# Loading the last pieces of batch 1 in row parts: a linear-attention kernel with a feed-forward layer on one Trainium2 core

## The chip, the cores and the metric

The kernel runs on one core of one Trainium2 chip. The metric is the time of one execution in microseconds (us) on the device; the figure for a kernel is the median of its runs. The profile is one further execution of the same program. Engines are called PE (matrix multiply; PEld is its weight load), DVE, ACT, POOL and SP (which here only issues transfers). "SPq" is SP's queue of transfer requests.

## The reference, cut to what matters

```python
# q, k, v: (batch 8, heads 8, seq 576, head_dim 64), float32
q_s = exp(q) / sum over head_dim          # softmax along d
k_s = exp(k) / sum over seq               # softmax along s
kv  = einsum('bhsd,bhse->bhde', k_s, v)
att = einsum('bhsd,bhde->bhse', q_s, kv)
x   = att.transpose(0, 2, 1, 3).reshape(4608, 512)
h   = x @ w_in                            # 512 -> 2048
g   = h + sin(alpha * h)**2 / alpha
out = g @ w_out                           # 2048 -> 512, float32
```

## The kernel before, in words

**Tiles.** The 4608 tokens are nine tiles `t` of 512. For each tile, `mm_h` (L282) makes sixteen blocks `ni` of 128 hidden features in PSUM, four matmuls for each; `sine` takes sin on ACT (L288) and squares it on ACT, POOL or DVE; `combine` (L298, DVE) adds and writes `g`; `mm_o` (L302) multiplies `g` by `wout`, 64 matmuls for a tile, and `evac_o` copies the result out of PSUM and stores it in two requests of 64 rows each (L317). The order on every engine is written out by hand.

**PSUM banks.** A block of `mm_h` takes the bank that its letter names. For tile 1 the sixteen letters are `"aabb..."` with a change in between:

```python
BANKS = {0: "aabbkllaabbkllaa", 1: "aakbbllaabbllaab", 2: "aabbopaabbopaabb"}
```

Letters a, b and l have two banks each, so the third block with a letter waits until `combine` of the first has read its bank. In tile 1, block 9 (b) so waits for `combine` of block 3, and block 15 (b) for that of block 9.

**Batch 1.** The attention of a batch makes the columns `xT` that `mm_h` reads. Batch 1's inputs are loaded in pieces into staging tiles `st_q`, `st_k`, `st_v` of 128 rows. `load_q1` (L466) loads q in two halves; `load_kv1` (L474) issues k's first half, v's first half, k's second half, and v's second half in two pieces: its first five groups of columns (`j` 0 to 5, 320 KB) and then its last four (256 KB). These five are called k0, v0, k1, v1a and v1b here. After them SP issues `wout_v` rows 14 and 15 into `late_w` (L491, 256 KB each; w14 and w15 here), the ninth q groups of batches 0 and 1 into `q8` (L493, 128 KB each), and then batch 2 with `load_batch(2)` (L99: q, k, v, 1152 KB each).

**Who uses them.** `cast_v1(1)` (L499) casts v1a on POOL and v1b on DVE into `vb`; `wide_mm(1, 1)` (L184) multiplies them with the exponential of k1. L545 casts w14 on POOL and w15 on ACT into `wout`; the last eight `mm_o` of tile 0 (`take(os)`, L553) need them. `exp_to` (L546, recorded at L118) takes the exponential of both parts of `q8` on ACT, and is followed on ACT by a table load (L552), one copy of `evac_o` and the sixteen sines of tile 1. `norm_q8` uses the result on DVE.

**The queue of requests.** All of these requests go through SP in program order. Their completion is told by eight semaphores (`DMAHW0` to `DMAHW7`) that are used in turn, and each request carries a wait on the semaphore that it is to use: it is issued when the request eight places before it has landed. A staging tile or `late_w` tile that is used again adds a wait for its last reader.

Of the kernel before, what the change touches and what calls it, by code (L numbers as in the profile page):

```python
# [23 lines left out]
def kernel(  # L24
# [14 lines left out]
    nc = tc.nc  # L39
    ctx.enter_context(nc.allow_non_contiguous_dma(reason="layout"))  # L40
    B, H, S, D = q.shape
# [3 lines left out]
    J = 9  # L45
# [23 lines left out]
    q8 = singles.tile([128, 4, 2, D], F32, name="q8")  # L69
# [9 lines left out]
    def src_view(t, b):  # L79
        return t[b].rearrange("(i e) (p j) d -> (e p) i (j d)", e=2, j=J)  # L80

    win_v = moe_w_in.rearrange("(c p) n -> p c n", c=4)
    wout_v = moe_w_out.rearrange("(no ni) d -> ni no d", ni=128)
    out_v = out.rearrange("(b p j) d -> b j p d", b=B, j=J)

    staged = {}
# [15 lines left out]
    def load_batch(b):  # L102
        load("q", q, b)
        load("k", k, b)
        load("v", v, b)
# [354 lines left out]
    with ES:  # L460
        def load_q1(ii):
            if ii == 0:
# [3 lines left out]
            nc.sync.dma_start(out=st[:, ii::2, 0:8].rearrange("p i j d -> p i (j d)"),  # L466
                              in_=src_view(q, 1)[:, ii::2, 0:8 * D])

        def load_kv1():
            for n in "kv":  # L470
                staged[n, 1] = stage.tile([128, 4, J, D], F32, name=f"st_{n}", tag="st")
            for n, t, ii, j0, j1 in (("k", k, 0, 0, J), ("v", v, 0, 0, J), ("k", k, 1, 0, J),
                                     ("v", v, 1, 0, 5), ("v", v, 1, 5, J)):
                nc.sync.dma_start(out=staged[n, 1][:, ii::2, j0:j1].rearrange("p i j d -> p i (j d)"),  # L474
                                  in_=src_view(t, 1)[:, ii::2, j0 * D:j1 * D])

        late = {6: lambda: load_q1(0), 8: lambda: load_wout(8, 12), 10: lambda: load_wout(12, 14),
                12: lambda: (load_q1(1), load_kv1())}
        for ni in range(nN):
            h_slot(0, ni, "DPPAPPAPPAAPPAPD"[ni], lag)  # L480
# [6 lines left out]
        os = o_quad(0, accs, [DVE_CP, ACT_CP, DVE_CP, DVE_CP])  # L487

        late_w = [spool.tile([128, MF], F32, name="s") for _ in range(2)]
        for n in range(2):  # L490
            nc.sync.dma_start(out=late_w[n], in_=wout_v[:, 14 + n])  # L491
        for b in range(2):
            nc.sync.dma_start(out=q8[:, :, b], in_=src_view(q, b)[:, :, 8 * D:J * D])  # L493
        load_batch(2)

        def cast_v1(ii):
# [157 lines left out]
    for ni in range(nN):  # L654
# [4 lines left out]
        elif ni in (9, 13):  # L659
            ii = ni // 12  # L660
# [3 lines left out]
    for t in range(3, nT):  # L664
        b = t + 1 if t + 1 < B else None
# [74 lines left out]
```

## Time and profile before

| | |
|---|---|
| runs | 281.94, 282.15, 282.15 us; median 282.15 us |
| the profiled execution's own time | 282.07 us |
| its span, first to last instruction | 280.3 us |
| granted TensorE clock | 0.997 |
| PE busy | 268.7 us |
| ACT, DVE, POOL busy | 224.1, 186.5, 81.1 us |
| moved by transfers | 46.06 MB, mean 164 GB/s |

The span is 1.77 us shorter than the execution's own time; what lies outside it is not part of the instructions. Times inside the profile count from the start of the span. A line of the timeline gives start, duration, engine, line, operation, tiles and, in brackets, how long the engine had been idle before it and what ended that idle time. A line of the waits gives the total, how often, and the longest.

### The profile page before, as it was taken

The page shows a single profiled execution, that of the slowest core. Times are in us where ns is not written, and L with a number is a line of the kernel's source. Part 1 is how long each engine was busy: PE and PEld are TensorE (multiplying, and loading weights), DVE is VectorE, ACT ScalarE, POOL GpSimd, SP SyncE. Part 2 cuts the span into 40 slices and gives each one's busy share as a digit, 9 for nine tenths or more (in the row PEclk, how much of TensorE's full clock was granted, in tenths as well). Part 3 has the DMA queues.
Part 4 walks back from the last instruction along what each step waited for, and adds up shares of the span by engine and source line. Part 5 has one row for each costly group of instructions (what it writes and reads, how often), then busy time and mean ns, then how long its engine had stood idle before and what let it go on. Part 6 is the DMA issues. An engine that isn't in the chain of part 4 may idle for free.

```text
span 280.3 us, 4775 instructions
## 1 busy us (share of the span) xinstructions
PE 268.7 (96%) x1814; PEld 124.9 (45%) x1843; DVE 186.5 (67%) x278; ACT 224.1 (80%) x321; POOL 81.1 (29%) x76
## 2 busy tenths in 40 slices
PE   3999999999999999999999999999999999999994
PEld 1544454444444444444444444444444444444443
DVE  3868877999779767766676677567775555555421
ACT  5799558999588999899989998999877777777400
POOL 2978112778666450026011600350000000000000
PEclk9999999999999999999999999999999999999998
DMA  7999999895698049712971199115001111111143
GB/s 257 313 197 235 291 384 404 269 401 144 140 269 343 0 104 302 301 39 66 328 309 39 40 294 365 44 39 124 18 21 37 37 40 40 41 42 44 39 99 75
DMA packets 39607, 46.06 MB, mean 164 GB/s; under 512 B 17040, under 2 KB 22944, under 8 KB 39584
## 3 DMA queue, kind: packets, MB, share of 16 engines
q1 hardware_dynamic: 33952, 41.11, 46.5%
q0 software_dynamic: 5472, 4.52, 9.7%
q8 instruction: 14, 0.23, 0.3%
q10 hardware_dynamic: 160, 0.13, 0.2%
q14 instruction: 9, 0.07, 0.1%
HBM read 36.71 MB, written 9.44 MB: 165 GB/s over the span
## 4 chain that ended last, share of the span: by engine, by line
PE 83%; DMA 6%; ACT 4%; issue 2%; POOL 1%; SPq 1%; DVE 1%; ACTq 0%
PE hp L282 37%; PE op L302 37%; DMA st_v<-in_v_dram 6%; ACT s L288 2%; PE kvp L173 2%; PE hp L302 2%; PE op L282 1%; PE op L710 1%; PE lp L282 1%; POOL s L292 1%; PE hp L237 1%; PE xp L237 1%; DVE g L298 1%; SPq L474 1%; SPq L327 0%
## 5 line engine op out<-in xcount | busy, mean ns | idle before, releaser
L298 DVE SCALAR_TENSOR_TENSOR g<-s,inva_sb,hp 128x512 bf16<-128x512 f32 x129 | 95.1, 745 | 58.9 <-ACT s L290 53.3
L282 PE MATMUL hp<-xT,win 128*128 128x512 bf16 x508 | 128.6, 379 | 0.5
L302 PE MATMUL op<-wout,g 128*128 128x512 bf16 x463 | 117.6, 379 | 1.7 <-issue 1.3
L288 ACT ACTIVATE s<-hp,alpha_sb 128x512 f32<-128x512 f32 x129 | 86.9, 684 | 21.7 <-PE hp L282 20.3
L282 PEld LDWEIGHTS <-win 128*128 128x128 bf16 x576 | 55.7, 98 | 67.8 <-issue 0.8
L302 PEld LDWEIGHTS <-g 128*128 128x128 bf16 x560 | 53.4, 98 | 65.0 <-issue 2.5
L290 ACT ACTIVATE s<-s 128x512 f32<-128x512 f32 x112 | 70.7, 632 | 3.6
L292 POOL TENSOR_TENSOR s<-s 128x512 f32<-128x512 f32 x28 | 29.5, 1066 | 16.3 <-ACT s L288 16.2
L152 POOL TENSOR_TENSOR qn<-qe,qs 128x1152 bf16<-128x1152 bf16 x11 | 23.2, 2128 | 28.8 <-DVE qs L146 24.4
L137 POOL CAST vb<-st_v 128x1152 bf16<-128x1152 f32 x12 | 14.7, 1258 | 46.1 <-DMA st_v<-in_v_dram 46.1
L314 DVE COPY o<-op 128x512 f32<-128x512 f32 (+2 forms) x32 | 21.1, 660 | 9.7 <-PE op L302 7.4
L118 ACT ACTIVATE qe<-st_q 128x1152 bf16<-128x1152 f32 (+2 forms) x18 | 17.7, 1027 | 6.0 <-DMA st_q<-in_q_dram 5.8
L118 ACT ACTIVATE ke<-st_k 128x1152 bf16<-128x1152 f32 x16 | 17.9, 1153 | 2.6 <-DMA st_k<-in_k_dram 2.6
L145 DVE TENSOR_REDUCE qs<-qe 128x36 f32<-128x2304 bf16 x5 | 12.8, 2551 | 8.3 <-ACT qe L118 8.3
L302 PE MATMUL hp<-wout,g 128*128 128x512 bf16 x45 | 12.0, 379 | 0.2 <-issue 0.2
L118 ACT ACT_TABLE_LOAD x7 | 9.0, 1283 | 0.8 <-PEq L724 0.7
L302 PE MATMUL lp<-wout,g 128*128 128x512 bf16 x32 | 9.2, 379 | 0.1
L371 PE MATMUL warm<-st_q,ident 128*128 128x512 f32 (+1 forms) x6 | 4.4, 871 | 4.5 <-DMA st_q<-in_q_dram 4.5
L282 PE MATMUL lp<-xT,win 128*128 128x512 bf16 x32 | 7.7, 379 | 0.5 <-DMA win<-in_moe_w_in_dram 0.5
L250 DVE CAST xT<-xp 128x1024 bf16<-128x1024 f32 (+1 forms) x7 | 7.4, 1065 | 0.0
L298 DVE SCALAR_TENSOR_TENSOR g<-s,inva_sb,lp 128x512 bf16<-128x512 f32 x8 | 5.7, 740 | 0.4 <-POOL s L292 0.4
L108 POOL DMA_DIRECT2D win<-in_moe_w_in_dram x8 | 5.9, 755 | 0.0
(99 smaller groups left out, 138.2 us busy)
## 6 DMA issues: line engine op xcount, KB each, us to landing
out_dram<-o SPq DMA_DIRECT2D x70, 128.0 KB, 2.4
st_q<-in_q_dram SPq DMA_DIRECT2D x6, 1152.0 KB, 6.6
st_k<-in_k_dram SPq DMA_DIRECT2D x6, 1152.0 KB, 9.2
st_v<-in_v_dram SPq DMA_DIRECT2D x6, 1152.0 KB, 11.5
st_k<-in_k_dram SPq DMA_DIRECT2D x4, 576.0 KB, 8.1
st_q<-in_q_dram SPq DMA_DIRECT2D x4, 512.0 KB, 6.0
wout<-in_moe_w_out_dram POOLq DMA_DIRECT2D x3, 512.0 KB, 11.6
win<-in_moe_w_in_dram POOLq DMA_DIRECT2D x5, 256.0 KB, 6.2
```

Source lines behind the costliest of these rows:

```text
L118: nc.scalar.activation(dst[:, :, ii * 128:(ii + 1) * 128].rearrange("p j (x d) -> p x j d", x=2), src[:, ii::2], AX.Exp)
L137: engs[ii](vv[:, 2 * ii:2 * ii + 2, :, 0:D], staged["v", b][:, ii::2])
L145: nc.vector.tensor_reduce(qs, A["qe", b].rearrange("p j (i d) -> p j i d", i=4), axis=AXL.X, op=ALU.add)
L152: engs[ii % len(engs)].tensor_tensor(qn[:, ii, 0:j1].rearrange("p j (x d) -> p j x d", x=2), qe[:, ii], part.unsqueeze(3).to_broadcast([12 ...
L250: eng(xT[:, c, d0:d0 + m - n], xp[..., n:m])
L282: nc.tensor.matmul(hp, win[:, KO[k], ni * 128:(ni + 1) * 128], xT[:, KO[k], t * MF % NX:t * MF % NX + MF], start=(k == 0), stop=(k == 3))
L288: nc.scalar.activation(s, hp, AX.Sin, scale=alpha_sb[:, ni:ni + 1])
L290: nc.scalar.activation(s, s, AX.Square)
L292: nc.gpsimd.tensor_tensor(s, s, s, op=ALU.mult)
L298: nc.vector.scalar_tensor_tensor(G[t][:, ni], in0=s, scalar=inva_sb[:, ni:ni + 1], in1=hp, op0=ALU.mult, op1=ALU.add)
L302: nc.tensor.matmul(acc, G[t][:, ni, j * 128:(j + 1) * 128], wout[:, ni, :], start=(ni == 0), stop=(ni == nN - 1))
L314: eng(o[:, cols], acc)
```

## The change

Five pieces are requested in two parts each, divided by rows (partitions) where they were one request of 128 rows: v1a in 104 and 24 rows, w14 in 120 and 8, w15 in 56 and 72, the ninth q groups of batch 0 in 88 and 40 and of batch 1 in 63 and 65. The order of the pieces, the bytes and the destinations stay. SP so issues five requests more. An instruction that reads one of these pieces now waits for the semaphores of both parts. The order of instructions on PE, DVE, ACT and POOL is unchanged.

```diff
+        def row_parts(*cuts):
+            at = (0,) + cuts + (128,)
+            return [slice(a, z) for a, z in zip(at, at[1:])]
+
         def load_kv1():
             for n in "kv":
                 staged[n, 1] = stage.tile([128, 4, J, D], F32, name=f"st_{n}", tag="st")
-            for n, t, ii, j0, j1 in (("k", k, 0, 0, J), ("v", v, 0, 0, J), ("k", k, 1, 0, J),
-                                     ("v", v, 1, 0, 5), ("v", v, 1, 5, J)):
-                nc.sync.dma_start(out=staged[n, 1][:, ii::2, j0:j1].rearrange("p i j d -> p i (j d)"),
-                                  in_=src_view(t, 1)[:, ii::2, j0 * D:j1 * D])
+            for n, t, ii, j0, j1, cuts in (("k", k, 0, 0, J, ()), ("v", v, 0, 0, J, ()), ("k", k, 1, 0, J, ()),
+                                           ("v", v, 1, 0, 5, (104,)), ("v", v, 1, 5, J, ())):
+                for r in row_parts(*cuts):
+                    nc.sync.dma_start(out=staged[n, 1][r, ii::2, j0:j1].rearrange("p i j d -> p i (j d)"),
+                                      in_=src_view(t, 1)[r, ii::2, j0 * D:j1 * D])
...
-        for n in range(2):
-            nc.sync.dma_start(out=late_w[n], in_=wout_v[:, 14 + n])
-        for b in range(2):
-            nc.sync.dma_start(out=q8[:, :, b], in_=src_view(q, b)[:, :, 8 * D:J * D])
+        for n, cut in ((0, 120), (1, 56)):
+            for r in row_parts(cut):
+                nc.sync.dma_start(out=late_w[n][r], in_=wout_v[r, 14 + n])
+        for b, cut in ((0, 88), (1, 63)):
+            for r in row_parts(cut):
+                nc.sync.dma_start(out=q8[r, :, b], in_=src_view(q, b)[r, :, 8 * D:J * D])
         load_batch(2)
```

## The prediction

> **What bounds the kernel now.** I read the page first, then the chain of work that ended last around the change (28 to 48 us), then SP's own waits, then the timeline of 38 to 60 us engine by engine, then busy time by windows.
>
> ```profile
> PE 268.7 (96%) x1814; PEld 124.9 (45%) x1843; DVE 186.5 (67%) x278; ACT 224.1 (80%) x321; POOL 81.1 (29%) x76
> ...
> sum 57.00, PE 56.26 PEld 26.34 DVE 48.11 ACT 45.05 POOL 30.18; mean PE 2.68 PEld 1.25 DVE 2.29 ACT 2.15 POOL 1.44
> ```
>
> PE is the bound. The second line is the sum over windows from 27 to 84 us: PE has 0.74 us of idle in 57. So a delay of PE here is not made up later, and a gain is limited to the few tenths that PE waits. The chain shows where it waits:
>
> ```profile
> 29.60 11.16 DMA st_v<-in_v_dram
> 40.76 0.05 issue
> 40.81 0.74 POOL vb L499
> 41.55 0.04 issue
> 41.59 0.77 PE kvp L184 x18
> 42.37 1.00 PE hp L282 x4
> ```
>
> v1a is issued at 29.60 and lands at 40.76; POOL casts it; PE's `wide_mm(1, 1)` starts on that. From 42.37 the chain is PE alone. The rest of the split pieces act on PE through ACT and DVE:
>
> ```profile
> 42.77 0.62 ACT L545 CAST wout<-s 128x512 bf16<-128x512 f32 x1 [0.97 <-DMA s<-in_moe_w_out_dram]
> 43.79 0.82 ACT L118 ACTIVATE qe<-q 128x256 bf16<-128x256 f32 x2 [0.40 <-DMA q<-in_q_dram]
> 48.35 1.41 DVE L298 SCALAR_TENSOR_TENSOR g<-s,inva_sb,hp 128x512 bf16<-128x512 f32 x2 [0.74 <-POOL s L292]
> 51.26 1.39 DVE L298 SCALAR_TENSOR_TENSOR g<-s,inva_sb,hp 128x512 bf16<-128x512 f32 x2
> 50.55 3.62 PE L282 MATMUL hp<-xT,win 128*128 128x512 bf16 x16
> ```
>
> ACT waits for w15, then for `q8`; from 43.79 it has no pause up to tile 1's first sine (46.50), whose square POOL hands to DVE at 48.35; DVE then has no pause either. The pair at 51.26 is `combine` of blocks 3 and 4: block 3 ends at about 51.95. The sixteen matmuls at 50.55 are blocks 7 to 10; one takes 0.216 us, so block 9, which reuses block 3's bank, starts at 52.28. **The margin is 0.33 us** (block 15 on block 9: 57.69 against 57.30, 0.39). If `q8` lands more than 0.33 us later, PE pays the rest.
>
> SP's waits:
>
> ```profile
> SPq L493 <- DMA st_k<-in_k_dram: 2.3, 1, 2.3
> SPq L99 <- DMA st_v<-in_v_dram: 0.7, 1, 0.7
> ```
>
> The second `q8` request stood 2.3 us, until k0 landed at 37.05: it is the eighth after k0. This is the wait of the semaphores used in turn, and the change moves it.
>
> Last, how dear a request of fewer than 128 rows is. The nearest rows are the stores of 64 rows, alone on the queue, against loads of 128 rows:
>
> ```profile
> 122.60:124.10 1.50, 1.50 (x9) 0.69 (x7) 0.38 (x1) 1.50 (x3) 0.00 (x0) 1.00 0.75 175
> 36.00:40.00 4.00, 4.00 (x46) 2.45 (x46) 3.50 (x5) 1.99 (x3) 0.62 (x1) 1.00 1.06 401
> ```
>
> The last two numbers are the transfer engines' busy share and GB/s: 175/0.75 = 233 against 401/1.06 = 378 GB/s for each unit of busy share. A byte in a 64-row request took 1.62 times as long.
>
> **The change, part by part.** The time of each piece on a full queue follows from the landings (issue plus time to landing: 40.76, 41.45, 42.13, 42.75, 43.22, 43.63): v1a 0.87 us after k1 (39.89), w14 0.68, w15 0.62, `q8` 0.47 and 0.41.
>
> *Cost of the parts.* Between nothing (same bytes, queue full) and 0.62 times these: 0.54, 0.42, 0.38, 0.29, 0.25, in all 1.88 us. A gain is the first rival. I take half, 0.31: 0.27, 0.21, 0.19, 0.15, 0.13, in all 0.95 us. Half, because the parts follow one another on a queue where engines are not in step, while the stores stood alone, and the `q8` pieces already move more slowly (131 KB in 0.41 to 0.47 us, against 262 KB in 0.62 to 0.68), which may hide the loss. [...]
>
> *v1a.* One more issue, 0.47 us, is covered: it stands at 29.60 and the queue reaches it near 39.9 (uncovered 0.5 us). Landing +0.27, POOL's cast and `wide_mm` follow: PE +0.27 at 41.59. v1b moves by the same, and with it the second half of `wide_mm`.
>
> *w14, w15.* Their second and later parts now wait for the second half of q (27.65 + 6.7 = 34.35), k0 (37.05) and v0 (38.45); w15 was out at 33.73. The queue reaches w15 after 42: covered by over 3 us. Landing: w14 42.61, w15 43.42 (+0.67). ACT's cast of w15 then ends at 44.07. PE wants w15 at 43.64 + 0.22 + 0.27 = 44.13: just covered.
>
> *q8.* Its four parts wait for k1 (39.89), v1a's two parts, and v1b (41.45 + 0.27 = 41.72). Issues take 0.42 and 0.68 in the trace, so the last is out at about 41.8 to 42.4. Issue to landing is at least 1.8 us in the stores (2.3 median), 43.6 to 44.7; by the queue 43.63 + 0.95 = 44.58. I take 44.58. ACT, POOL and DVE move by 0.95; PE loses 0.95 - 0.33 = 0.62, which contains the 0.27 of v1a (PE waits for the later one). Three further semaphore waits on ACT at 17 ns each (the row of L317's) make 0.05.
>
> *Batch 2.* SP's three requests go out at about 42.4 instead of 38.51, 3.9 us late behind the `q8` waits. q, k and v landed at 46.5, 49.3 and 52.8; ACT first reads q at 61.33 and POOL v at 61.08: 8.3 us of cover for v. The first store, which stood 2.8 us behind them, has no reader; uncovered it would hold an `o` buffer, of which there are four.
>
> Sum: 0.62 + 0.05, rounded to **0.7 us**: 282.07 + 0.7 = 282.8 us for the profiled execution; the median of the runs is 0.08 higher, within the rounding.
>
> **The rivals.**
>
> *The parts leave out a late engine (no change, or faster).* The trace's completion records raise each request's semaphore sixteen times. For v1a fifteen lie between 38.49 and 39.43 and one at 40.76; every request from k0 to `q8` has one such straggler, 0.9 to 1.3 us late. If the straggler has no share of the parts, v1a lands at 39.43 + 0.2 and PE starts `wide_mm` when it is free (41.45 instead of 41.59) and does not pause for DVE's cast (0.06): about -0.2 us, **281.9**. `q8` then lands within its margin. It decides from the point where v1a lands before 40.6. For: the straggler is there, and v1a's landing heads the chain. Against: nothing in the profile says that the parts avoid it, or which engine it is; and PE has only 0.3 us to give. [...]
>
> *The wait in turn decides (slower by more).* If each `q8` issue takes 0.7 us and the last (42.7) lands 2.3 later, at 45.0, PE loses 45.0 - 43.63 - 0.33 = 1.05: **283.1**. A `q8` request in the trace took 6.6 us to land, but behind a full queue; this one would be near its head.
>
> *All is hidden.* The parts cost nothing in a full queue, `q8` lands within 0.33: 282.1 to 282.3.
>
> **How the numbers follow.** A measurement of this kernel can tell about 0.2%, 0.56 us. Forecast 0.50: its spread is 0 to 1.56 us (1.88 - 0.33), so 0.42 slower, 0.08 same. Straggler rival 0.28: 0.19 same, 0.09 faster. Wait in turn 0.12: slower. Hidden 0.08: same. 0.02 for what I do not see, half each way. In all: faster 0.10, same 0.35, slower 0.55. The range goes from the straggler rival with all of PE's 0.3 us (281.8) to the forecast's upper end (283.6). The forecast's own range, by its two bounds, is 282.1 to 283.6.
>
> **What would show it.** Right: v1a's cast on POOL later than 40.81, ACT's exponential of `q8` near 44.7, DVE's first `combine` of tile 1 near 49.3, and a PE wait on DVE between 50 and 58 us that was not there. The straggler rival: POOL's cast before 40.5 and `q8` at or before 43.8. The wait in turn: the last `q8` issue after 42.5 with an empty queue behind it. I am wrong at the root if `q8` is late by over 0.5 us and PE still loses nothing, or if PE loses time outside 38 to 60 us.

## Result and profile after

| | before | changed |
|---|---|---|
| median of nine runs each | 282.02 us (281.64 to 282.28) | 283.94 us (283.27 to 285.9) |
| the profiled execution's own time | 282.07 us | 283.37 us |
| its span | 280.3 us | 281.6 us |
| granted TensorE clock | 0.997 in the profiled execution | 0.998 in the profiled execution; of the nine runs, 0.998 to 1.000 in five, 0.992 to 0.993 in four |

The ratio is 1.0083, interval 1.0067 to 1.0098: slower by 1.9 us, where 0.7 was forecast. The direction was right; the size was not, and the median is 0.34 above the range. The five runs at full clock lie between 283.27 and 283.94, and their median, 283.83, is still 1.81 us above the kernel before; the four others, at 284.76 to 285.9, have no profile, and why their clock is lower stays open.

The page of the changed kernel, in the line of busy times, has no more work on any engine than before (PE's sum differs because matmul records are missing in the trace of before):

```profile
PE 272.3 (97%) x1843; PEld 125.3 (44%) x1843; DVE 186.5 (66%) x278; ACT 223.6 (79%) x321; POOL 80.5 (29%) x76
```

So the time is a wait. The chain that ended last (start, duration, what) shows whose:

```profile
31.46 11.43 DMA st_v<-in_v_dram
42.90 0.02 issue
42.92 0.44 DVE vb L506
43.36 0.04 issue
43.40 0.40 PE kvp L184 x8
43.81 1.00 PE hp L282 x4
```

Before, it came through v1a and POOL's cast; now it comes through v1b, which the change does not touch. `mm_h` goes on at 43.81 instead of 42.37. PE's timeline at this place, with the idle time and its releaser in brackets, first the kernel before, then the changed one:

```profile
41.59 0.77 PE L184 MATMUL kvp<-vb,ke 64*128 64x130 bf16 x18
42.65 0.46 PE L184 MATMUL kvp<-vb,ke 64*128 64x130 bf16 x10 [0.77 <-POOL vb L506]
43.40 0.40 PE L184 MATMUL kvp<-vb,ke 64*128 64x130 bf16 x8 [0.29 <-DVE vb L506]
```

Before, the eighteen matmuls ran in one piece, with 0.10 us of idle ahead of them. The timelines of ACT, POOL and DVE give the landings. Two lines of the kernel before, for k1 and v1b (the prediction shows the others):

```profile
39.91 1.17 ACT L118 ACTIVATE ke<-st_k 128x1152 bf16<-128x1152 f32 x1 [0.70 <-DMA st_k<-in_k_dram]
41.48 0.43 DVE L499 CAST vb<-st_v 128x512 bf16<-128x512 f32 x1 [0.77 <-DMA st_v<-in_v_dram]
```

The changed one:

```profile
41.20 1.16 ACT L118 ACTIVATE ke<-st_k 128x1152 bf16<-128x1152 f32 x1 [1.61 <-DMA st_k<-in_k_dram]
41.87 0.73 POOL L506 CAST vb<-st_v 128x640 bf16<-128x640 f32 x1 [2.37 <-DMA st_v<-in_v_dram]
42.92 0.43 DVE L506 CAST vb<-st_v 128x512 bf16<-128x512 f32 x1 [1.83 <-DMA st_v<-in_v_dram]
44.22 0.62 ACT L552 CAST wout<-s 128x512 bf16<-128x512 f32 x1 [1.39 <-DMA s<-in_moe_w_out_dram]
45.60 0.72 ACT L118 ACTIVATE qe<-q 128x256 bf16<-128x256 f32 x2 [0.76 <-DMA q<-in_q_dram]
```

The first of these lines matters most: k1 is one whole request, issued ahead of every part, and ACT starts on it at 41.20 where it was 39.91. Then v1a on POOL comes 1.06 later, v1b on DVE 1.44, w15 1.45 and `q8` 1.81. About 0.4 us of each may not be the change's: in this execution q's second half is already requested 0.47 later (28.12 against 27.65), and `wide_mm(1, 0)` starts 0.39 later (39.74 against 39.35). A second profile of the same kernel (e10 below) requests it at 27.53, and there v1 is 1.7 us late all the same. From `wide_mm(1, 1)` on the delay is simply carried: the late `xp` matmul of tile 1 stands at 60.11 instead of 58.64 (+1.47).

The windows from 38 to 44 us (the last two numbers are the transfer engines' busy share and GB/s), first the kernel before:

```profile
38.00:44.00 6.00, 5.74 (x66) 2.92 (x66) 3.94 (x10) 3.54 (x6) 1.97 (x3) 1.00 1.09 379
```

then the changed one:

```profile
38.00:44.00 6.00, 4.94 (x59) 2.43 (x58) 3.88 (x8) 2.67 (x4) 1.96 (x3) 1.00 0.91 228
43.00:44.00 1.00, 0.71 (x13) 0.34 (x9) 1.00 (x3) 0.00 (x0) 0.60 (x1) 1.00 0.59 137
```

The engines are busy nearly as much (0.91 against 1.09) and move 228 instead of 379 GB/s. The second line shows that the queue also runs empty at the end. SP's waits say why:

```profile
SPq L500 <- DMA st_k<-in_k_dram: 2.0, 1, 2.0
SPq L500 <- DMA st_v<-in_v_dram: 0.6, 1, 0.6
```

The four parts of `q8` go out at 41.19, 41.54, 41.99 and 42.91, behind the landings of k1, v1a and v1b; batch 2 follows at 43.41 to 44.45.

### The profile page after: what moved, and what is told of

Its sections match the earlier page's. It is cut to its first block, busy times and chain, and to the rows that moved or that the text cites. A ratio compares the mean times of both kernels' runs of the same rounds, so it can differ in the third digit from the quotient of the medians.

```text
span 281.6 us, 4814 instructions
## 1 busy us (share of the span) xinstructions
PE 272.3 (97%) x1843; PEld 125.3 (44%) x1843; DVE 186.5 (66%) x278; ACT 223.6 (79%) x321; POOL 80.5 (29%) x76
## 4 chain that ended last, share of the span: by engine, by line
PE 87%; DMA 5%; ACT 3%; POOL 1%; SPq 1%; issue 1%; DVE 1%; ACTq 0%
PE op L302 37%; PE hp L282 37%; DMA st_v<-in_v_dram 4%; ACT s L288 2%; PE warm L371 2%; PE hp L302 2%; PE kvp L173 2%; DMA st_q<-in_q_dram 1%; PE op L282 1%; PE op L717 1%; PE lp L282 1%; POOL s L292 1%; SPq L479 1%; PE hp L237 1%; PE xp L237 1%
## 5 line engine op out<-in xcount | busy, mean ns | idle before, releaser
L302 PE MATMUL op<-wout,g 128*128 128x512 bf16 x480 | 120.4, 379 | 0.0
L137 POOL CAST vb<-st_v 128x1152 bf16<-128x1152 f32 x12 | 14.0, 1194 | 45.1 <-DMA st_v<-in_v_dram 45.1
L302 PE MATMUL hp<-wout,g 128*128 128x512 bf16 x48 | 12.7, 380 | 0.0
```

Of the source, the lines that this page charges most:

```text
L137: engs[ii](vv[:, 2 * ii:2 * ii + 2, :, 0:D], staged["v", b][:, ii::2])
L302: nc.tensor.matmul(acc, G[t][:, ni, j * 128:(j + 1) * 128], wout[:, ni, :], start=(ni == 0), stop=(ni == nN - 1))
```

## The experiments

The theories in short. A: the lateness of v1 at `wide_mm` sets the loss; its first form (A1) blames the unequal shares of the sixteen transfer engines, its second (A2) the fact that a request of adjacent rows is slow. B: the lateness of `q8` sets it. C: each further request costs, whatever its rows. Each kernel ran beside runs of the kernel before on the same chip; the ratios are against these.

### One part of the change alone: e1_v1a_only, e2_w_q_only

```diff
 e1: w14, w15 and q8 whole
-for n, cut in ((0, 120), (1, 56)):
+for n, cuts in ((0, ()), (1, ())):
-for b, cut in ((0, 88), (1, 63)):
+for b, cuts in ((0, ()), (1, ())):
 e2: v1a whole
-("v", v, 1, 0, 5, (104,))
+("v", v, 1, 0, 5, ())
```

> Only v1a is split (104 and 24 rows); w14, w15 and q8 are whole. Theory A (the parts make v1a and v1b late, and PE waits for the two casts before wide_mm of batch 1): most of the loss stays, 1.0 to 1.8 us slower than the kernel before, v1a's cast on POOL 0.6 to 1.0 us later, v1b's on DVE over 0.7 later. Theory B (the ten requests together, through the semaphores used in turn and q8, make the loss): under 0.4 us slower, q8's exponential no later than 44.2. Theory C (each further request costs, whatever its rows): a fifth of the loss, 0.4 us.

> v1a is whole; w14, w15 and the two q8 pieces are split as in the change. Theory A: PE does not pay, within 0.4 us of the kernel before; v1a's cast stays at 40.8, q8's exponential comes 0.7 to 1.2 us later than 43.8 and PE has 0.33 us of margin for it, so 0 to 0.6. Theory B: 1.3 to 1.9 us slower. Theory C: four fifths of the loss, 1.5 us.

e1: 282.62 against 281.99 us, ratio 1.0031 (1.0013 to 1.0049). e2: 282.76, ratio 1.0032 (1.0016 to 1.0049). That is 0.63 and 0.77 us: each part alone costs a third or a little more of the whole, and none of the three theories has both right. In e1 k1 is late (ACT at 40.78) and `mm_h` goes on at 43.07, where the timeline of before has 42.30. In e2 v1a and v1b are whole and yet late; the timeline of e2:

```profile
41.34 0.73 POOL L506 CAST vb<-st_v 128x640 bf16<-128x640 f32 x1 [2.27 <-DMA st_v<-in_v_dram]
42.19 0.43 DVE L506 CAST vb<-st_v 128x512 bf16<-128x512 f32 x1 [1.47 <-DMA st_v<-in_v_dram]
```

0.53 and 0.71 later than before, by parts that stand behind them in the queue.

### Same number of requests, other cuts: e3_all_64, e4_v1a_cols

```diff
 e3: each of the five pieces in 64 and 64 adjacent rows
-(104,)   (0, 120), (1, 56)   (0, 88), (1, 63)
+(64,)    (0, 64), (1, 64)    (0, 64), (1, 64)
 e4: v1a in two requests of 128 rows, by columns; the rest whole
+for i in ((slice(1, 2), slice(3, 4)) if j1 == 5 else (slice(ii, 4, 2),)):
```

> All five pieces are split 64 and 64: as many requests as in the change, the parts equal. Theory A1 (the loss comes from parts that give some engines more rows than others): within 0.3 us of the kernel before. Theory A2 (it comes from parts of fewer than 128 rows moving more slowly, 1.62 times as long for a byte in the 64-row stores): v1a 0.3 to 0.6 us late, 0.5 to 1.5 us slower. Theory C: as slow as the change, 1.9 us.

> v1a is split by head pairs: two requests of 128 rows and half the columns each; the rest is whole. One request more than before, no part by rows. Theories A1 and A2: no loss, within 0.2 us of the kernel before. Theory C: 0.4 us slower, and as slow as the kernel with v1a alone split by rows.

e3: 284.33 us, ratio 1.0079 (1.0061 to 1.0097). With equal parts the loss is at least as large (2.3 us against 1.9), so unequal shares (A1) are not what causes it; it is also larger than A2 expected. e4: 281.95, ratio 0.9995 (0.9984 to 1.0007): a second request of 128 rows costs nothing here, where the second request in e1 costs 0.6 us. It is not the request but its rows. In e3 `mm_h` goes on at 43.83, 1.53 late; `q8` is 2.65 late (46.44) and the `xp` matmul 2.30 (60.94): the margin is 0.35, and the rest of PE's loss is `q8`'s. SP can begin with its four requests only at k1's landing (40.74), the last waits for v1b's too (42.98), and it goes out at 43.46, when the third (1.32 us long) is done:

```profile
43.46 0.62 SPq L500 DMA_DIRECT2D q<-in_q_dram  x1
```

By the completion records the three other parts have all landed at 45.04; this one lands at 46.33, 2.87 after its issue. Here the late request sets `q8`'s lateness.

### The q8 path: e5_q8_whole, e6_q8_only

```diff
 e5: v1a, w14, w15 as in the change, q8 whole
-for b, cut in ((0, 88), (1, 63)):
+for b, cuts in ((0, ()), (1, ())):
 e6: only q8 as in the change
-for n, cut in ((0, 120), (1, 56)):
+for n, cuts in ((0, ()), (1, ())):
-("v", v, 1, 0, 5, (104,))
+("v", v, 1, 0, 5, ())
```

> v1a, w14 and w15 are split as in the change, q8 is whole. Theory A (PE pays through the two casts of v1, and q8 stays within its margin): as slow as the change, 1.3 to 2.2 us slower than the kernel before; DVE's cast of v1b 1.0 to 1.6 us later than 41.48. Theory B (q8's late landing is what PE pays, as the prediction's sum had it): under 0.7 us slower.

> Only the two q8 pieces are split. Theory A: within 0.3 us of the kernel before; v1's casts stay at 40.8 and 41.5; q8's exponential comes 0 to 0.5 us later. Theory B: 0.6 us slower or more.

e5: 283.58 against 281.81 us, ratio 1.0054 (1.0037 to 1.0070). e6: 283.04, ratio 1.0037 (1.0022 to 1.0051). The chain of e6 is the one that the prediction described:

```profile
45.85 0.40 ACT qe L118
...
50.65 0.73 DVE g L298
51.39 0.92 DVE s L294
52.31 1.33 DVE g L298 x2
53.64 0.04 issue
53.68 1.89 PE hp L282 x8
```

v1's casts are on time (40.01 and 40.73), `q8` starts at 45.52 (+1.73), and block 9 waits for the combine of block 3; the `xp` matmul is 1.39 late, so the margin is 0.34. Theory A's claim that `q8` costs nothing falls. The losses do not add: 1.8 us in e5, 1.2 in e6, 1.9 with all parts. PE waits for the later path, and after a late `wide_mm` most of `q8`'s lateness is hidden. e5 does not take `q8`'s lateness away, though: in its profile (282.74 us, the quickest of its six runs) v1b's cast comes at 42.23, 0.75 late and less than A expected, and `q8`, whole but behind slow pieces, starts at 45.00, 1.21 late. Less the margin that is 0.88, and the `xp` matmul is 0.89 late (59.53). In e6 the `q8` parts are issued early, at 34.71 to 39.10, and the last lands at 45.03: here the lateness is not the wait in turn.

### What slows the whole pieces: e7_w14_whole, e8_steady_v

```diff
 e7: v1a and w14 whole, w15 and q8 as in the change
-("v", v, 1, 0, 5, (104,))
+("v", v, 1, 0, 5, ())
-for n, cut in ((0, 120), (1, 56)):
+for n, cuts in ((0, ()), (1, (56,))):
 e8: the kernel before, with v of batches 5, 6, 7 (each behind whole q and k) in row parts
+V_ROWS = {("v", 5): ((0, 64), (64, 128)), ("v", 6): ((32, 96), (0, 32), (96, 128)),
+          ("v", 7): ((0, 104), (104, 128))}
```

> v1a and w14 are whole; w15 and q8 are split. In the run with v1a whole but w14, w15 and q8 split, v1's casts came 0.5 and 0.7 us late although v1 itself was untouched. Theory N (engines that are ahead and work on the row parts slow those that are still on the whole pieces before): with w14 whole in between, the engines ahead reach the parts only when the last is done with v1: casts at 40.8 to 41.0 and 41.5 to 41.7, and within 0.3 us of the kernel before, though w15 and q8 land as late as there. Theory S (the requests themselves, more of them waiting in SP's queue, slow v1): casts as late as there, 41.3 and 42.2, and 0.7 us slower.

> The kernel before, but v of batches 5, 6 and 7 (1152 KB each, each behind whole q and k and needed much later) is requested in parts: batch 5 in rows 0 to 63 and 64 to 127; batch 6 in rows 32 to 95, then 0 to 31, then 96 to 127; batch 7 in 0 to 103 and 104 to 127; batch 4 stays whole, 2.8 us after k's landing. [...] Theory E (any request of fewer than 128 rows is slow by the same factor of 1.6): 2.2 us for each 64-row part, rows 32 to 95 as well, 4.5 us in all for batches 5 and 7. Theory Q (parts are slow only where engines are out of step, as at 40 us): 1.4 us for each 64-row part, 2.8 to 3.1 us in all everywhere.

e7: 282.18 us, ratio 1.0009 (0.9997 to 1.0020). One whole piece between v1 and the first parts brings nearly all of the time back: POOL's cast of v1a starts at 40.75; DVE's cast of v1b, at 41.81, is still 0.33 late. So the whole pieces in e2 were slowed by transfer engines that had gone ahead to the row parts of w14, whose completions begin there at 40.74, before v1b's last at 42.17 (theory N; S falls). That one completion stands for one engine is the author's reading; no trace names the engine.

One thing in e7 came otherwise than expected: w15 and `q8` are in the same parts as in e2, and the `q8` parts are those of e6, but `q8` starts at 44.00, 0.21 late, where it was 0.84 late in e2 (44.63) and 1.73 in e6. The completion records suggest why. w14 has fifteen completions by 40.98 and the last at 42.70; w15's first part ends at 42.87, but the twelve of its second part are in by 42.69 and the first `q8` part by 43.06. So the late engine seems to have no share of w15's second part: here the parts do leave it out, as the first rival said, and that hides their price. It is read from the times, not tested; it means that the 1.2 us of e6 are not the price of the `q8` rows alone.

e8 took 282.03 us in one run. The windows of its loads: v of batch 4 whole, batch 5 in rows 0 to 63 and then 64 to 127, batch 6's first part (rows 32 to 95), batch 7's rows 0 to 103.

```profile
87.50:90.20 2.70, 2.70 (x16) 1.01 (x14) 2.70 (x4) 2.17 (x4) 1.68 (x2) 1.00 0.93 369
113.50:118.90 5.40, 5.24 (x31) 2.21 (x30) 4.09 (x9) 4.38 (x7) 0.00 (x0) 1.00 1.06 221
142.00:143.40 1.40, 1.40 (x13) 0.42 (x10) 1.24 (x3) 1.37 (x3) 0.00 (x0) 1.00 1.03 400
171.30:176.20 4.90, 4.74 (x28) 2.00 (x27) 3.83 (x7) 3.90 (x7) 0.00 (x0) 1.00 0.93 202
```

For each unit of busy share that is 397, 208, 388 and 217 GB/s. Sixty-four adjacent rows run here at about half the rate of whole v when they are the lower and then the upper half (208 against 397), and at nearly the full rate when they are rows 32 to 95 (388); so E and Q fall. Whole k of batch 5, ahead of the halves, fits theory N too: fifteen of its completions come by 113.52 and the last at 118.74, where k of batch 4, ahead of a whole v, has them by 88.19 and at 89.50 (q's last was late too, by 2.2 us against 0.2). Rows 0 to 103 hold rows of both halves, and yet they run at little more than half the rate, 217. Why uneven parts such as v1a's 104 rows are this slow stays open; lying in one half of the 128 is not the whole reason.

### The same requests with spread rows: e9_even_odd, e10_changed_again, e11_even_odd_q8_whole

```diff
 e9: all five pieces in even rows and odd rows; e11: v1a, w14, w15 so, q8 whole
-at = (0,) + cuts + (128,)
-return [slice(a, z) for a, z in zip(at, at[1:])]
+return [slice(0, 128, 2), slice(1, 128, 2)] if cuts else [slice(0, 128)]
```

e10 is the changed kernel again, beside e9.

> All five pieces are still requested in two parts of 64 rows, as in the run with 64 and 64 adjacent rows (284.33 us), but one part takes the even rows and the other the odd ones. [...] Theory P (what a request costs hangs on which rows it holds together, and adjacent rows that lie in one half of the 128 move at half rate): rows spread over all 128 move at full rate, so the loss is gone: POOL's cast of v1a at about 40.8, DVE's cast of v1b at about 41.5, the q8 exponential at 43.8 to 44.2 (only the semaphores used in turn are left), time 281.9 to 282.4, ratio 1.000 to 1.002. Rival R (two requests of half the rows are dear by themselves, whichever rows): as with adjacent rows, POOL's cast near 41.9, q8 near 46.4, 284.3 us, ratio 1.008.

> The changed kernel itself, beside the run with even and odd rows on the same chip. All theories: 283.3 to 284.2 us, ratio 1.006 to 1.008, with wide_mm pausing for DVE's cast of v1b. Open: in four of the nine executions seen so far the granted clock was 0.992 to 0.993 and the time about 1 us more; if that belongs to the change, it appears again here in some of the executions, and if it was the chip, it does not.

> v1a, w14 and w15 in two parts each as even and odd rows, the ninth q groups whole. The run with the same three pieces in adjacent rows and q8 whole took 283.58 us (ratio 1.0054). With all five pieces in even and odd rows v1's casts were on time (40.23 and 40.94) but q8 came at 45.20, and it took 282.91. Theory P (adjacent rows in one half of the 128 are the price of v1a, w14 and w15; what was left with even and odd rows is q8's path alone): no loss, 281.7 to 282.2 us, ratio 0.999 to 1.001, v1's casts at 40.2 to 40.9 and 40.9 to 41.5, q8 exponential by 44.1. Rival (the three additional requests cost by themselves, through SP or the queue): 282.5 to 283, as with all five in even and odd rows.

e9: 282.91 against 281.82 us, ratio 1.0032 (1.0020 to 1.0045). e10: 283.67, ratio 1.0090 (1.0056 to 1.0123). e11: 282.3 against 281.9, ratio 1.0007 (0.9994 to 1.0020), with v1's casts at 40.90 and 41.46 and `q8` at 44.10, 0.31 late and so within the margin: its `xp` matmul stands at 58.64, where it was before. The clean comparison is e3 with e9, which differ only in which rows go together: v1's casts come at 41.91 and 43.01 in e3 and at 40.23 and 40.94 in e9, and the ratio falls from 1.0079 to 1.0032. That shows the cause of the v1 loss. e11 beside e5 (1.0054) agrees, though there the sizes of the parts differ too. Windows from 38 to 41 us, while v1 is on its way, of e10 and of e9:

```profile
38.00:41.00 3.00, 3.00 (x38) 1.54 (x36) 2.17 (x5) 0.82 (x3) 0.62 (x1) 1.00 1.06 244
```

```profile
38.00:41.00 3.00, 3.00 (x35) 1.43 (x33) 2.71 (x6) 1.69 (x2) 2.05 (x2) 1.00 1.03 375
```

| | before | changed | e1 | e2 | e3 | e4 | e5 | e6 | e7 | e9 | e10 | e11 |
|---|---|---|---|---|---|---|---|---|---|---|---|---|
| GB/s for each unit of busy share, 38 to 41 us | 348 | 258 | 251 | 335 | 247 | 370 | 243 | 369 | 367 | 364 | 230 | 368 |
| ACT starts on k1, us | 39.91 | 41.20 | 40.78 | 39.86 | 40.77 | 39.91 | 40.69 | 39.11 | 39.77 | 39.24 | 40.93 | 39.93 |

All kernels with v1a in adjacent rows stand at 230 to 258 and start on k1, whole and ahead of it, at 40.69 or later; all others stand at 335 and more and start on k1 by 39.93.

What was missed is e9's `q8`, expected near 44 and found at 45.20. Here the wait in turn did act: the first part waits for k1 (39.22), the four issues follow one another at about 0.66 us, and the last goes out at 41.23, when the queue is nearly empty; fifteen of its sixteen completions come by 43.91, 0.28 later than q8's last before. The sixteenth comes at 45.09, and that decides. The trace has a 16 KB packet of the kind "instruction" at 43.08 that takes 0.95 us, ahead of it; in the kernel before this packet comes at 44.43, after `q8`. That it delayed this engine is read from the times, not tested; the trace does not tell which engine moves a packet.

```profile
45.20 0.72 ACT L118 ACTIVATE qe<-q 128x256 bf16<-128x256 f32 x2 [1.98 <-DMA q<-in_q_dram]
```

In e10 two of seven runs (285.9 and 286.51 us) again have a clock of 0.992 and 0.994. With the first nine that makes six of sixteen runs of this kernel, one of twelve of e2, and none of the 81 runs of the kernel before that stand beside the experiments (0.997 at the least). So it seems to come with the change; by what, stays open. In e10's profile, at a clock of 0.998, the loss is `wide_mm` alone:

```profile
43.31 0.79 PE L184 MATMUL kvp<-vb,ke 64*128 64x130 bf16 x18 [1.84 <-POOL vb L506]
```

## Why the prediction was right and wrong

**PE has no slack: right.** What `wide_mm` loses is still there at 60 us (+1.44, then +1.47) and in the span (+1.3).

**The margin of `q8`, 0.33 us: right.** Lateness of `q8` less lateness of the `xp` matmul is 0.35 in e3, 0.34 in e6 and 0.34 in e9 (1.41 and 1.07), and in e11 0.31 costs nothing. In the changed kernel itself the predicted PE wait on DVE between 50 and 58 us did not appear, since PE was already later: block 9 could start at 52.00 + 8 × 0.216 = 53.73, and combine of block 3 ended near 53.70. That is a near tie: `q8`'s lateness less the margin is 1.81 - 0.33 = 1.48, and `wide_mm` had lost 1.44.

**The cost of the parts: this is the step that failed.** Half of the measured factor was taken, 0.31 where the stores gave 0.62, because the parts would overlap on a queue where engines are out of step; for v1 that made 0.27 us. Measured, v1b landed at 42.90 instead of 41.45, 1.45 late (1.74 in e10, at 43.19). The factor was too small: in e8, behind whole requests, halves of adjacent rows cost a factor of 1.9 (397 against 208 GB/s a unit), above the stores' 1.62. But the full price of v1a's own 0.87 us is 0.54 by the stores' factor and 0.79 by e8's (0.87 × 0.91), and this still falls short of 1.45; the rest is the next point.

**Who pays: wrong, by the same step.** The price was charged to the parts alone. It falls on whole requests that are on their way beside them too: k1, ahead of every part, came 1.29 late (0.87 in e1), and v1b in e2 0.71 late. In the changed kernel the packets of 2304 bytes that start between 38 and 41 us, the last of k1 among them, take 132 ns on average instead of 93 (162 in e1, 122 in e10, 93 in e2), and those of v1b (1024 bytes) 68 at the median instead of 46. So v1's lateness was 1.06 for the cast on POOL and 1.44 on DVE (1.72 and 1.73 in e10) instead of 0.27, and "PE loses 0.62, which contains the 0.27 of v1a" came out the other way round: PE lost 1.4 to 1.7 at `wide_mm`, and that contains nearly all of `q8`'s.

**`q8`: later than the sum, and by another way.** It was 1.81 late (1.99 in e10) instead of 0.95. The sum took the queue to decide. But the last part could be requested only when v1b had landed, at 42.90 instead of the 41.72 that was expected, and it landed at 45.40, 2.49 after its issue:

```profile
42.91 0.31 SPq L500 DMA_DIRECT2D q<-in_q_dram  x1
```

In e2 and e10, too, the last request goes out within 0.01 us of v1b's landing (42.17 and 43.19), and it lands 2.27 later in both. So 1.81 is near the 1.88 of the upper end by luck; most of it is v1b's lateness, passed on by the wait in turn.

**w15 and batch 2.** w15's cast ended at 44.84, after the 44.13 that was allowed, but PE had moved by 1.4 itself. Batch 2's k and v landed 2.7 and 2.1 us later than before, and no engine paused for them: this cover was right.

**The straggler rival: wrong for the changed kernel.** The late engine was not left out of v1a: of the thirteen completions that v1a's first part has, twelve come by 40.03 and the last at 41.50; of the twelve of its second part, eleven by 40.57 and the last at 41.74. So counted, the ten parts (104, 24, 120, 8, 56, 72, 88, 40, 63 and 65 rows) have 13, 12, 15, 8, 14, 12, 11, 10, 9 and 13 completions, where a whole piece has sixteen; one earlier record of each part, 0.45 to 1.51 us after its issue, is left out of the count, and the others come 1.57 us after the issue or later. Which engines take part, the trace does not tell. The one part of the changed kernel that seems to leave the late engine out is the 8-row part of w14, all in by 42.59 when the part of 120 rows ends at 43.34. In e7, with other pieces whole, the rival's mechanism seems to have been at work.

**The wait in turn: in part right.** The last issue came after 42.5 (42.91; 43.20 in e10, 43.46 in e3) and the queue ran empty, which is this rival's sign. Its sum, with the measured landing of 45.40, gives 45.40 - 43.63 - 0.33 = 1.44, about PE's loss; but in the changed kernel `wide_mm` had lost as much already, so the wait explains `q8`'s lateness there and not the time. In e3 the late last request adds 0.8 us to what `wide_mm` lost, and in e9 it acts with a straggler. In e6, with the parts issued by 39.41, `q8` is late without it. Other semaphores for these requests were not tried.

## What to carry to other kernels

A load that must be split should be split by columns (e4, ratio 0.9995) or by alternate rows (e11, 1.0007), which cost nothing here, not by adjacent rows (e3, 1.0079); rows 0 to 103 were slow too (217 GB/s a unit of busy share, 397 for a whole load), although they hold rows of both halves (e8). Price a slow request at its full measured factor at least (1.9 in e8), and charge it to every transfer that is in flight beside it, those ahead of it in the queue included (k1, 1.29 us late), and to the requests that wait for its semaphore (the last `q8` part, out at 42.91); one whole request of 256 KB between the urgent piece and the slow ones was nearly enough of a fence here (e7, 1.0009). When two late inputs feed one busy engine, as here, the later one is paid and the other is hidden, so undoing one of them returns little (1.8 us left in e5, 1.2 in e6, of 1.9).

## What the hardware showed that was not expected

Engines that are done with a piece went on to later requests before the others were done (in e2 w14's completions begin at 40.74, v1b's last is at 42.17), and where these are adjacent rows, the pieces still under way were slower (DVE's cast of v1b 0.71 late in e2, 0.33 in e7; k1 at 40.69 or later with v1a in adjacent rows, by 39.93 in all others). Rows 32 to 95 moved at 388 GB/s a unit of busy share and rows 0 to 63 with 64 to 127 behind them at 208 (e8). One 16 KB packet of the kind "instruction", 0.93 us long before and 1.24 in the changed kernel, falls among these loads, and where it falls moved from 44.43 to 42.42 us with the change. No version here is faster than the kernel before: e4 and e11 equal it (ratios 0.9995 and 1.0007).
